# New durations for three kinds of operation in the planner that orders a fused attention and feed-forward kernel, and new due times

## The chip, the cores and the metric

The kernel runs on one core of one Trainium2 chip. The metric is device time in microseconds (us) of one execution. A core has five engines with a queue each: TensorE (PE, with its weight loads listed apart as PEld), VectorE (DVE), ScalarE (ACT), GpSimd (POOL) and SyncE (SP, which here only issues DMAs). An engine works its own queue in order; engines meet through semaphores. The kernel before takes 650.52 us, the median of three runs from 650.5 to 650.76 us.

## The reference

Three stages, all in fp32, on 2 x 768 tokens:

```
scores = (q @ k.T) / 8 + bias(distance) ; keep local window of 96 and 8 global columns
a      = softmax(scores)                ; x = a @ v              8 heads of 64
x      = (x @ w_a) * (x @ w_b) @ w_out                           512 -> 1536 -> 512
h      = x @ w_in ; g = h if h >= 1, 0 if h <= -1, else (h + 1)^2 / 4
out    = g @ w_out2                                              512 -> 2048 -> 512
```

The feed-forward weights are float64 arrays. The kernel makes two fp32r tiles of each, a high and a low part, and does every product of these stages as three matmuls (high by high, high by low, low by high).

## The kernel before, in words

**Work.** The 1536 tokens are three tiles of 512. Attention is cut into 24 *units*, eight to a tile: one pair of heads and 256 queries. Here they are numbered 0 to 23 in the order in which they run. A unit has four PE steps: *scores* (L730), a *turn* for each of its two heads (transposes of the softmax rows, L801) and *values* (L818). Between them lie, per unit, four reductions on DVE that read the scores from PSUM (L754), four exponentials on ACT (L766), one addition of four numbers on ACT (L774), a reciprocal on DVE (L777), four *norms* (softmax rows times the reciprocal: L97 on ACT, L99 on DVE or POOL), two copies of the turned rows out of PSUM (L432 on ACT, L434 on DVE), and a split of the values' result into the high and low part of x (a cast, then L693). The q of each unit is scaled first (L97 or L99 too).

**Weights.** Each of 68 weight tiles arrives raw by DMA and goes through seven operations: Abs on ACT (L421), four bit operations on DVE (L422 to L425; the first may go to POOL), a cast to the high part (L432 or L434) and a subtraction for the low part (L427, DVE or POOL).

**Products.** The feed-forward stages are 2460 matmuls of 128 x 128 weights by 512 columns: `early` (L641) does the first 48, for tile 0, interleaved by column block of x, and `run` does the others (L489 and L518).

**What sets the order.** Nothing is scheduled on the chip. While the program is built, `Clock` replays the kernel with a table of durations and writes each queue in the order that this replay reaches. `on` enters an operation with a due time (now plus a slack by kind, `SLACK`) and a duration for each engine that may do it; `one` gives it to the engine that would end first, with a surcharge for DVE (`BIAS`). `write` and `product` advance PE's clock by the modelled length of a step. The loop at L1043 to L1069 chooses between the next product and the next attention step, by how far attention is behind its share (`behind`, `AHEAD`, `LATE`, `RUN`, `OVER`) and in the order of steps in `ORDER`. Before the first product PE gets filler matmuls (L1066) wherever the replay has nothing for it. On the chip the durations are what they are: a duration in the table that is wrong puts an operation at a wrong place or on a wrong engine, and the queues wait for each other there.

**Tables that matter below.** `NORM` and `NORM1` (L63, L64): the norm of 256 and of 128 columns and the scaling of q, 270 and 165 ns on ACT. The duration of Abs (L421): 520 ns. `TURNED` and the length of a turn (L60, L808). `FIRST` (L44): the loads issued before the replay begins. `UNITS` (L704): how many units may be between scores and values, which is also the depth of the row pools.

Of the kernel before, what the change touches and what calls it, by code (L numbers as in the profile page):

```python
# [15 lines left out]
AF = mybir.ActivationFunctionType  # L16
# [4 lines left out]
P = 128  # L21
# [19 lines left out]

NQ = 2

FIRST = ((0, 0), (0, 1), (2, 0), (0, 2), (1, 0), (2, 1), (0, 3), (1, 1), (2, 2), (1, 2), (2, 3))  # L44

AHEAD_QK, AHEAD_V = 4, 3

# [9 lines left out]
MM = 227  # L57


ENTER, TURNED, LEAVE = 95, 174, 107  # L60
COPY = dict(scalar=520, vector=335)
COPY_PS = dict(scalar=478, vector=602)
NORM = dict(scalar=270, vector=262)  # L63
NORM1 = dict(scalar=165, vector=198)  # L64
SUB = dict(vector=602, gpsimd=1225)
CLAMP = dict(vector=335, gpsimd=1883)

BIAS = dict(any=150, weights=400, norm=150, q=150)

HOP = dict(tensor=200, scalar=160, vector=170, gpsimd=120)  # L70
DMA = dict(issue=580, begin=1600, rate=260, end=900)
# [1 line left out]
BEFORE = 5450  # L73

SLACK = dict(
    qk=0, reduce=-1500, exp=1500, share=-3000, norm=-1000, turn=-3000, x=-1000, evac=0, mid=0, y=2000, weights=4500, soon=1900,
)


GAP = dict(first=0, att=3000, later=3966, soon=26)  # L80

AHEAD = 40


RUN, LATE, OVER = 3, 12, 8

ORDER = "stv"


def as_f32(ap):  # L90
    return ap.bitcast(F32)
# [38 lines left out]
class Clock:  # L130
# [7 lines left out]
    def __init__(self, nc):  # L138
        self.nc = nc
        self.now, self.seq, self.events = 0, 0, []  # L140
        self.busy = dict.fromkeys(self.ENGINES, 0)
        self.port = 0
        self.line = []
        self.dma_issue = self.dma_busy = -1 << 20
        self.poll = lambda: None

        self.att = None
# [5 lines left out]
    def on(self, slack, emit, then=None, need=None, port=True, bias="any", **costs):  # L153


        self.seq += 1
        bisect.insort(self.line, (self.now + slack, self.seq, costs, port, BIAS[bias], emit, then, need))

# [35 lines left out]
                gate = at + ns  # L194
        return False

    def dma(self, n, then):
        issued = max(self.dma_issue, self.now)
        self.dma_issue = issued + DMA["issue"]
        self.dma_busy = max(self.dma_busy, issued + DMA["begin"]) + n / DMA["rate"]  # L200
        self.after(self.dma_busy + DMA["end"] - self.now, then)

    def product(self, ns):

        ns += LEAVE if self.att else 0
        self.att = None
        return ns

# [20 lines left out]
class Loads:  # L229
# [34 lines left out]
    def more_raw(self, u, clock):  # L264

        first = max(n for what, n in FIRST if what == 2)
        for n in range(u + NRAW if u else first + 1, u + NRAW + 1):
# [40 lines left out]
    def dma(self, clock, dst, src, then=lambda: None):  # L308
        n = 4
        for k in dst.shape:  # L310
            n *= k
        self.nc.sync.dma_start(dst, src)
        if clock:
            clock.dma(n, then)
        else:
            self.first.append((n, then))

    def begin(self):
        first = {0: self.load, 1: self.load_v, 2: self.load_raw}
        for what, n in FIRST:  # L320
            first[what](n)

    def follow(self, clock):

        clock.now = -BEFORE
        for n, then in self.first:
            clock.dma(n, then)
        clock.now = 0


class Ffn:
# [3 lines left out]
    def __init__(self, ctx, tc, clock, loads, out, half):  # L335
# [27 lines left out]
        self.early_ps, self.begun = [], False  # L363
        self.gap = GAP["first"]
        self.room = dict(ab=2, acc=2, s1=2, s2=2)
# [28 lines left out]
    def prep(self, urgent):  # L394
        clock = self.clock
        u = self.n_prep
        self.n_prep += 1
        r = self.loads.raw(u)
        low, high = r[:, :, 0], r[:, :, 1]
        b = self.p_bits.tile([P, T], U32, tag="bits", name=f"bits{u}")  # L400
        wh, wl = self.slots.pop(0)
        self.used.append(u)
        self.in_flight += 1
        slack = SLACK["soon" if urgent else "weights"]

        def chain(*steps):
            (emit, costs), rest = steps[0], steps[1:]

            def then():
                if rest:  # L410
                    chain(*rest)
                else:
                    self.loads.more_raw(u, clock)
                    self.w[u] = wh, wl
                    self.in_flight -= 1

            clock.on(slack, emit, then, bias="weights", **costs)

        shl, shr, both, or_ = ALU.logical_shift_left, ALU.logical_shift_right, ALU.bitwise_and, ALU.bitwise_or
        chain(  # L420
            (lambda e: e.activation(as_f32(b), as_f32(high), AF.Abs), dict(scalar=520)),  # L421
            (lambda e: e.tensor_scalar(as_f32(b), as_f32(b), HUGE, TINY, ALU.min, ALU.max), CLAMP),  # L422
            (lambda e: e.tensor_scalar(b, b, 3, 0x3FFFFFF8, shl, both), dict(vector=335)),
            (lambda e: e.scalar_tensor_tensor(b, low, 29, b, shr, or_), dict(vector=602)),  # L424
            (lambda e: e.scalar_tensor_tensor(b, high, 0xC0000000, b, both, or_), dict(vector=602)),  # L425
            (lambda e: self.copy(e, wh, as_f32(b)), COPY),
            (lambda e: e.tensor_tensor(wl, as_f32(b), as_f32(wh), ALU.subtract), SUB),  # L427
        )
# [181 lines left out]
    def prepare(self):  # L610

        if self.can_prep() and self.n_prep in self.loads.have:
            urgent = self.first_use[self.n_prep] - self.now < GAP["soon"]
            if urgent or self.clock.now - self.prep_at >= self.gap:
# [42 lines left out]
class Attention:  # L657
# [15 lines left out]
    def write(self, ns, then, turn=False):  # L673

        if not turn:
            ns += {None: ENTER, "turn": TURNED, "other": 0}[self.clock.att]
        self.clock.att = "turn" if turn else "other"
        self.clock.after(ns + HOP["tensor"], then)
        self.clock.advance(ns)
# [18 lines left out]
class Window(Attention):  # L698
# [2 lines left out]

    UNITS = 3  # L704

    def __init__(self, ctx, early, tc, clock, ffn, loads, ident, masks, scales):
        super().__init__(ctx, tc, clock, ffn, ident)
# [36 lines left out]
    def reduce(self, st, j, r, ps):  # L744
# [34 lines left out]
        def norms():  # L779
            for jj in range(2):  # L780
                for rr in range(NQ):
                    clock.on(SLACK["norm"], *self.norm(st, jj, rr), bias="norm", gpsimd=457, **(NORM if self.places(st)[rr][1] > P else NORM1))

# [11 lines left out]
    def turn(self, st, j):  # L795

        clock, pt = self.clock, st["p", j]
        n = sum(w for _, w in self.places(st))
        ps = self.take()
        for c in range(0, n, P):  # L800
            self.nc.tensor.transpose(ps[:, c : c + P], pt[:, c : c + P], self.ident)  # L801

        def out():
            self.give(ps)
            st["turned", j] = True

        copy = lambda e: self.ffn.copy(e, pt[:, :n], ps[:, :n])
        self.write(146 + 52 * n // P, lambda: clock.on(SLACK["turn"], copy, out, None, False, scalar=20 + n * 9 // 10, vector=n * 7 // 6), True)  # L808

    def values(self, st):  # L810

# [18 lines left out]
    def steps(self):  # L830
# [6 lines left out]
        def score(n):  # L837
            self.scores(units[n])
            if n + 1 < len(units):
                nxt = units[n + 1]  # L840
                here = lambda: nxt.update(qs=True)
                scale = lambda e: loads.scale(e, n + 1, self.scales)
                self.clock.on(SLACK["qk"], scale, here, lambda: "here" in nxt, bias="q", gpsimd=453, **NORM)

# [127 lines left out]
def tile_kernel(ctx: ExitStack, tc: tile.TileContext, nn, qz, k2, qd, kd, vd, wu, out):  # L972
# [54 lines left out]
    with tc.If(near != 0, preferred_fallthrough_block=True) as cmp:  # L1027
        with ExitStack() as arm:
# [14 lines left out]
            while holds:  # L1043
# [4 lines left out]
                if step and (  # L1048
# [4 lines left out]
                    if done == per_tile:  # L1053
                        ffn.gap = GAP["att"]
                    if not any(steps.values()):
# [134 lines left out]
```

## Time and profile before

| | |
|---|---|
| time, median of 3 runs | 650.52 us |
| the profiled execution | 650.85 us |
| its span, first to last instruction | 648.9 us |
| around the span | 1.95 us |
| PE busy | 637.9 us (98%) |
| DVE busy | 444.3 us (68%) |
| ACT busy | 262.1 us (40%) |
| POOL busy | 62.9 us (10%) |

The shares are means over stretches with different limits: attention is in the first 130 us, and from there on the products have PE to themselves. PE's busy time counts filler matmuls and overlapped ends as well. A row of a timeline gives the start, the duration, the engine, the line, the operation and its tiles; where instructions of one engine overlap at their ends, the time that one costs the engine is the distance from its start to the next one's start.

### The profile page before, as it was taken

How to read it: one execution, taken by the hardware profiler on the slowest of the kernel's cores; microseconds unless marked ns; L12 is line 12 of the kernel's file. 1: busy time of each engine (PE TensorE's matmuls, PEld its weight loads, DVE VectorE, ACT ScalarE, POOL GpSimd, SP SyncE). 2: the span in 40 equal slices, each digit the busy share in tenths (PEclk: the TensorE clock that was granted, in tenths of full speed). 3: DMA queues.
4: the chain of work that ended last, by engine and by line, in shares of the span. 5: the costliest groups of instructions: out<-in, count | busy, mean ns of one | idle time of the engine just before them, and what ended most of it. 6: DMA issues, size and time to landing. Idle time of an engine off the chain costs nothing.

```text
span 648.9 us, 8928 instructions
## 1 busy us (share of the span) xinstructions
PE 637.9 (98%) x3211; PEld 516.0 (80%) x3211; DVE 444.3 (68%) x970; ACT 262.1 (40%) x611; POOL 62.9 (10%) x82
## 2 busy tenths in 40 slices
PE   8899999999999999999999999999999999999997
PEld 4567777888888888888888888888888888888886
DVE  7999976364943838943949978685879587744442
ACT  6999989723421213301313435452434133211110
POOL 1112211000000000000000011000010211022220
PEclk9999999999999999999999999999999999999999
DMA  7776652022320303410302411230213120000112
GB/s 241 224 227 197 203 150 87 17 66 66 106 89 0 130 0 98 130 32 1 129 2 88 130 43 66 66 97 33 65 66 96 35 66 0 1 0 17 48 51 86
DMA packets 23765, 52.70 MB, mean 81 GB/s; under 512 B 3104, under 2 KB 11552, under 8 KB 23712
## 3 DMA queue, kind: packets, MB, share of 16 engines
q1 hardware_dynamic: 23568, 52.05, 26.0%
q8 instruction: 27, 0.44, 0.3%
q14 instruction: 26, 0.21, 0.1%
q10 hardware_dynamic: 144, 0.00, 0.0%
HBM read 48.89 MB, written 3.15 MB: 80 GB/s over the span
## 4 chain that ended last, share of the span: by engine, by line
PE 88%; ACT 2%; issue 0%; DVE 0%; ACTq 0%
PE ps L489 48%; PE o L518 20%; PE y L518 15%; PE at L801 2%; PE at L818 2%; PE at L730 1%; ACT p L766 1%; ACT p L432 0%; ACT p L97 0%; PE e L641 0%; ACT bits L421 0%; DVE ab L549 0%; ACT w_hlh L432 0%; ACT a L432 0%; DVE opart L607 0%
## 5 line engine op out<-in xcount | busy, mean ns | idle before, releaser
L566 ACT ACTIVATE c<-c,half 128x512 f32<-128x512 f32 x48 | 34.7, 724 | 139.1 <-DVE c L563 139.0
L489 PE MATMUL ps<-xlx,w_hlh 128*128 128x512 f32 x224 | 87.5, 390 | 0.0
L489 PE MATMUL ps<-xhx,w_hlh 128*128 128x512 f32 x224 | 87.4, 390 | 0.0
L489 PE MATMUL ps<-xhx,w_hll 128*128 128x512 f32 x224 | 87.4, 390 | 0.0
L563 DVE TENSOR_SCALAR c<-ps 128x512 f32<-128x512 f32 x48 | 33.0, 688 | 51.6 <-PE ps L489 51.5
L489 PE MATMUL ps<-xhy,w_hlh 128*128 128x512 f32 x168 | 65.4, 389 | 0.0
L489 PE MATMUL ps<-xly,w_hlh 128*128 128x512 f32 x168 | 65.4, 389 | 0.0
L489 PE MATMUL ps<-xhy,w_hll 128*128 128x512 f32 x168 | 65.4, 389 | 0.0
L549 DVE TENSOR_TENSOR ab<-ps,a 128x512 f32<-128x512 f32 x34 | 23.4, 687 | 56.5 <-PE ps L489 56.3
L432 ACT CAST w_hlh<-bits 128x512 fp32r<-128x512 f32 x50 | 31.0, 622 | 49.4 <-DVE bits L425 44.8
L571 DVE TENSOR_TENSOR g<-ps,c 128x512 f32<-128x512 f32 x48 | 33.0, 688 | 25.1 <-ACT c L566 24.8
L489 PEld LDWEIGHTS ps<-xhx,w_hlh 128*128 128x128 f32 x224 | 42.0, 188 | 9.0 <-issue 0.3
L489 PEld LDWEIGHTS ps<-xhx,w_hll 128*128 128x128 f32 x224 | 42.1, 188 | 8.9 <-issue 0.2
L489 PEld LDWEIGHTS ps<-xlx,w_hlh 128*128 128x128 f32 x224 | 42.1, 188 | 8.7 <-issue 0.2
L421 ACT ACTIVATE bits<-raw 128x512 f32<-128x512 f32 x68 | 43.9, 668 | 8.6 <-DVE w_hll L427 5.3
L425 DVE SCALAR_TENSOR_TENSOR bits<-raw,bits 128x512 uint32<-128x512 uint32 x68 | 46.3, 691 | 0.6
L424 DVE SCALAR_TENSOR_TENSOR bits<-raw,bits 128x512 uint32<-128x512 uint32 x68 | 45.7, 683 | 0.5
L432 ACT COPY a<-ps 128x512 f32<-128x512 f32 x22 | 12.9, 589 | 81.2 <-PE ps L489 81.0
L518 PE MATMUL o<-w_hlh,midl 128*128 128x512 f32 (+1 forms) x101 | 39.1, 387 | 0.0
L518 PE MATMUL o<-w_hll,midh 128*128 128x512 f32 (+1 forms) x101 | 39.1, 387 | 0.0
L518 PE MATMUL o<-w_hlh,midh 128*128 128x512 f32 (+1 forms) x101 | 39.1, 387 | 0.0
L427 POOL TENSOR_TENSOR w_hll<-bits,w_hlh 128x512 fp32r<-128x512 f32 x11 | 14.8, 1350 | 235.4 <-ACT w_hlh L432 212.1
(316 smaller groups left out, 1392.6 us busy)
## 6 DMA issues: line engine op xcount, KB each, us to landing
raw<-in_wu SPq DMA_DIRECT2D x68, 512.0 KB, 3.6
v<-in_vd SPq DMA_DIRECT2D x16, 256.0 KB, 3.0
k<-in_k SPq DMA_DIRECT2D x16, 200.0 KB, 2.9
q<-in_qd SPq DMA_DIRECT2D x48, 64.0 KB, 3.6
out<-opart SPq DMA_DIRECT2D x11, 256.0 KB, 2.0
k<-in_k SPq DMA_DIRECT2D x8, 128.0 KB, 3.6
v<-in_vd SPq DMA_DIRECT2D x8, 128.0 KB, 3.7
v<-in_vd SPq DMA_DIRECT2D x8, 64.0 KB, 2.7
```

What stands on the lines that cost most here:

```text
L421: (lambda e: e.activation(as_f32(b), as_f32(high), AF.Abs), dict(scalar=520)),
L424: (lambda e: e.scalar_tensor_tensor(b, low, 29, b, shr, or_), dict(vector=602)),
L425: (lambda e: e.scalar_tensor_tensor(b, high, 0xC0000000, b, both, or_), dict(vector=602)),
L427: (lambda e: e.tensor_tensor(wl, as_f32(b), as_f32(wh), ALU.subtract), SUB),
L432: e.copy(dst, src)
L489: nc.tensor.matmul(ps, l, r, start=c == 0 and m == 0, stop=last)
L518: nc.tensor.matmul(ps[:, cols], l, r[:, cols], start=f == lo and m == 0, stop=last)
L549: e.tensor_tensor(ab[0], ps, self.a.pop((t, f)), ALU.mult)
L563: e.tensor_scalar(c[0], ps, -1.0, 1.0, ALU.max, ALU.min)
L566: e.activation(c[0], c[0], AF.Square, bias=self.half, scale=0.5)
L571: e.tensor_tensor(g[0], ps, c[0], ALU.max)
L801: self.nc.tensor.transpose(ps[:, c : c + P], pt[:, c : c + P], self.ident)
```

## The change

Line numbers of the changed kernel are 2 to 5 higher. It does five things: it sets the durations of ACT's scaled copy and of Abs higher and models the turns differently, it sets the due times and some limits anew, it issues one raw weight tile less before the replay (`FIRST`), it lets four units be under way (`UNITS`), and it brings in a second DMA queue that stays unused (`ALONG = 0`, so `queue` is always that of SP).

```diff
-FIRST = ((0, 0), (0, 1), (2, 0), (0, 2), (1, 0), (2, 1), (0, 3), (1, 1), (2, 2), (1, 2), (2, 3))
+FIRST = ((0, 0), (0, 1), (2, 0), (0, 2), (1, 0), (2, 1), (0, 3), (1, 1), (1, 2), (2, 2))
+ALONG = 0
-ENTER, TURNED, LEAVE = 95, 174, 107
+ENTER, LEAVE, TURNED = 95, 107, 25
-NORM = dict(scalar=270, vector=262)
-NORM1 = dict(scalar=165, vector=198)
+NORM = dict(scalar=400, vector=262)
+NORM1 = dict(scalar=292, vector=198)
-BIAS = dict(any=150, weights=400, norm=150, q=150)
+BIAS = dict(any=150, weights=150, norm=400, q=150)
...
-    qk=0, reduce=-1500, exp=1500, share=-3000, norm=-1000, turn=-3000, x=-1000, evac=0, mid=0, y=2000, weights=4500, soon=1900,
+    qk=400, reduce=0, exp=1500, share=-3000, norm=0, turn=-3000, x=1000, evac=1000, mid=2000, y=2000, weights=1500, soon=1900,
...
-AHEAD = 40
-RUN, LATE, OVER = 3, 12, 8
-ORDER = "stv"
+AHEAD = 16
+RUN, LATE, OVER = 1, 24, 8
+ORDER = "tsv"
...
-        ns += LEAVE if self.att else 0
+        ns += {None: 0, "turn": TURNED, "other": LEAVE}[self.att]
...
+            queue = sum(q for _, _, q in self.first) < ALONG and len(self.first) % 2
+            (self.nc.scalar if queue else self.nc.sync).dma_start(dst, src)
...
-            (lambda e: e.activation(as_f32(b), as_f32(high), AF.Abs), dict(scalar=520)),
+            (lambda e: e.activation(as_f32(b), as_f32(high), AF.Abs), dict(scalar=560)),
...
-            ns += {None: ENTER, "turn": TURNED, "other": 0}[self.clock.att]
+            ns += 0 if self.clock.att == "other" else ENTER
...
-    UNITS = 3
+    UNITS = 4
...
-        self.write(146 + 52 * n // P, lambda: clock.on(SLACK["turn"], copy, out, None, False, scalar=20 + n * 9 // 10, vector=n * 7 // 6), True)
+        self.write(109 * n // P, lambda: clock.on(SLACK["turn"], copy, out, None, False, scalar=20 + n * 9 // 10, vector=n * 7 // 6), True)
```

**Where instructions go.** In all, 24 fewer operations of the window path stand in ACT's queue, 14 fewer in DVE's, and 38 more in POOL's. Three places show how.

ACT's queue from unit 1's addition (`st_2_0`) on, before. `p_2_0` and `p_0_1` are the softmax rows of units 1 and 2 (the last number is the head), `q_71` the q of unit 3, `bits` a weight tile in preparation, `at` a PSUM bank of attention:

```order
L774 ACTIVATE st_2_0__296<-st_2_0__296 128x4
L766 ACTIVATE p_0_1_0_331,st_0_1__330<-p_0_1_0_331,st_0_1__330 128x256
L97 ACTIVATE q_71<-q_71,scales 128x256
L97 ACTIVATE p_2_0_0_297<-p_2_0_0_297,st_2_0__296 128x256
L97 ACTIVATE p_2_0_1_298<-p_2_0_1_298,st_2_0__296 128x256
L421 ACTIVATE bits_362<-raw_62 128x512
L766 ACTIVATE p_0_1_1_332,st_0_1__330<-p_0_1_1_332,st_0_1__330 128x128
L766 ACTIVATE p_0_1_1_332,st_0_1__330<-p_0_1_1_332,st_0_1__330 128x256
L432 COPY p_2_0_0_297<-at_264 128x512
L774 ACTIVATE st_0_1__330<-st_0_1__330 128x4
```

The same place in the changed kernel:

```order
L779 ACTIVATE st_2_0__296<-st_2_0__296 128x4
L771 ACTIVATE p_0_1_0_330,st_0_1__329<-p_0_1_0_330,st_0_1__329 128x256
L771 ACTIVATE p_0_1_1_331,st_0_1__329<-p_0_1_1_331,st_0_1__329 128x128
L771 ACTIVATE p_0_1_1_331,st_0_1__329<-p_0_1_1_331,st_0_1__329 128x256
L426 ACTIVATE bits_361<-raw_62 128x512
L779 ACTIVATE st_0_1__329<-st_0_1__329 128x4
L99 ACTIVATE p_2_0_1_298<-p_2_0_1_298,st_2_0__296 128x256
L437 COPY p_2_0_0_297<-at_265 128x512
L99 ACTIVATE p_0_1_0_330<-p_0_1_0_330,st_0_1__329 128x128
L99 ACTIVATE p_0_1_0_330<-p_0_1_0_330,st_0_1__329 128x256
L99 ACTIVATE p_0_1_1_331<-p_0_1_1_331,st_0_1__329 128x256
```

The scaling of q and one of unit 1's norms have left the queue, and unit 2's exponentials stand ahead of the norm that remains; unit 2's norms follow close by.

POOL's queue from its first operation inside the window path, before:

```order
L99 TENSOR_SCALAR p_2_0_0_297<-p_2_0_0_297,st_2_0__296 128x256
L422 TENSOR_SCALAR bits_362<-bits_362 128x512
L99 TENSOR_SCALAR p_0_1_0_331<-p_0_1_0_331,st_0_1__330 128x256
L99 TENSOR_SCALAR p_2_1_0_394<-p_2_1_0_394,st_2_1__393 128x256
L99 TENSOR_SCALAR p_2_1_1_395<-p_2_1_1_395,st_2_1__393 128x256
L99 TENSOR_SCALAR p_0_2_0_479<-p_0_2_0_479,st_0_2__478 128x256
L99 TENSOR_SCALAR q_71<-q_71,scales 128x256
L427 TENSOR_TENSOR w_hll_212<-bits_492,w_hlh_211 128x512
```

The same place in the changed kernel:

```order
L101 TENSOR_SCALAR q_70<-q_70,scales 128x256
L101 TENSOR_SCALAR p_0_0_0_277<-p_0_0_0_277,st_0_0__276 128x256
L101 TENSOR_SCALAR p_2_0_0_297<-p_2_0_0_297,st_2_0__296 128x256 x2
L101 TENSOR_SCALAR p_2_0_1_298<-p_2_0_1_298,st_2_0__296 128x256
L432 TENSOR_TENSOR w_hll_205<-bits_309,w_hlh_204 128x512
L101 TENSOR_SCALAR p_0_1_1_331<-p_0_1_1_331,st_0_1__329 128x128
L101 TENSOR_SCALAR q_69<-q_69,scales 128x256
L101 TENSOR_SCALAR p_2_1_0_387<-p_2_1_0_387,st_2_1__386 128x256
L101 TENSOR_SCALAR p_2_1_1_388<-p_2_1_1_388,st_2_1__386 128x256
```

The norms of unit 0 to 3 that left ACT and DVE, and more of the q scalings, are on POOL now, two or three in a row, and so is the subtraction of the first weight tile (`w_hll`).

PE's queue from the last scores ahead of unit 6's turns to its first values (`p_0_3`), before. The `e` tiles are the PSUM banks of the first 48 products, `xhx` and `xlx` the two parts of x:

```order
L730 MATMUL at_264<-k_75,q_68 128x256
L801 MATMUL at_263<-ident,p_0_3_0_554 128x128 x3
L641 MATMUL e_273<-xhx_1_366,w_hlh_205 128x512
L641 MATMUL e_273<-xlx_1_367,w_hlh_205 128x512
L641 MATMUL e_273<-xhx_1_366,w_hll_206 128x512
L801 MATMUL at_265<-ident,p_0_3_1_555 128x128 x3
L641 MATMUL e_274<-xhx_1_366,w_hlh_207 128x512
L641 MATMUL e_274<-xlx_1_367,w_hlh_207 128x512
L641 MATMUL e_274<-xhx_1_366,w_hll_208 128x512
L818 MATMUL at_263<-p_0_3_0_554,v_82 64x128
```

The same place in the changed kernel, from the first of these turns on:

```order
L806 MATMUL at_262<-ident,p_0_3_0_530 128x128 x3
L646 MATMUL e_274<-xhx_0_364,w_hlh_208 128x512
L806 MATMUL at_265<-ident,p_0_3_1_531 128x128 x3
L646 MATMUL e_274<-xlx_0_365,w_hlh_208 128x512
L735 MATMUL at_263<-k_76,q_69 128x128
L735 MATMUL at_262<-k_76,q_69 128x128
L735 MATMUL at_263<-k_76,q_69 128x256
L735 MATMUL at_262<-k_76,q_69 128x256
L823 MATMUL at_265<-p_0_3_0_530,v_82 64x128
```

Six products stood between and behind the two turns, and two stand there now; a unit's scores have moved in behind the turns. Up to unit 6's first values PE has had 18 products before and has had 8 now.

## Rows read from the trace of the kernel before

**Rows 1.** Windows: busy us (and instructions) of each engine, clock, DMA

```profile
6.00:22.00 16.00, 13.67 (x114) 9.35 (x113) 13.84 (x55) 14.94 (x54) 1.58 (x3) 1.00 0.84 263
22.00:30.00 8.00, 7.42 (x58) 4.92 (x58) 7.91 (x35) 7.95 (x28) 1.86 (x4) 1.00 0.86 277
30.00:100.00 70.00, 67.97 (x515) 50.14 (x516) 62.69 (x209) 66.87 (x217) 13.65 (x17) 1.00 0.65 188
130.00:640.00 510.00, 510.00 (x2252) 422.25 (x2251) 339.90 (x590) 145.44 (x236) 41.44 (x32) 1.00 0.19 59
```

**Rows 2.** Groups by line: filler matmuls, count, busy us, mean ns

```profile
L1066 PE MATMUL e<-ident 128*128 128x256 bf16 x21 | 3.3, 274 | 0.0
```

**Rows 3.** Waits of PE, 6 to 130 us: total us, times, longest

```profile
PE at L730 <- ACT q L97: 1.6, 2, 1.0
PE at L801 <- ACT p L97: 1.5, 3, 0.6
PE at L818 <- ACT p L432: 1.1, 3, 0.5
PE at L801 <- DVE xlx L693: 0.5, 1, 0.5
```

**Rows 4.** Timeline of ACT: operations that start one behind another

```profile
14.26 0.50 ACT L97 ACTIVATE q<-q,scales 128x256 f32<-128x256 f32 x1
14.66 0.90 ACT L97 ACTIVATE p<-p,st__296 128x256 f32<-128x256 f32 x2
...
18.48 1.10 ACT L97 ACTIVATE p<-p,st__330 128x128 f32<-128x128 f32 x3
19.47 0.50 ACT L766 ACTIVATE p<-p,st__393 128x256 f32<-128x256 f32 x1
...
19.96 0.36 ACT L432 CAST xhx<-at 128x256 fp32r<-128x256 f32 x1
20.21 0.48 ACT L432 COPY p<-at 128x384 f32<-128x384 f32 x1
```

**Rows 5.** Timeline: additions of units 0 and 15 on ACT

```profile
9.70 0.19 ACT L774 ACTIVATE st__277<-st__277 128x4 f32<-128x4 f32 x1
...
77.40 0.24 ACT L774 ACTIVATE st__1104<-st__1104 128x4 f32<-128x4 f32 x1
```

**Rows 6.** Timeline of PE: first scores, then values of units 6 and 15

```profile
5.74 1.34 PE L730 MATMUL at<-k,q 64*128 64x128 f32 x8
...
40.90 1.01 PE L818 MATMUL at<-p,v 128*64 128x128 f32 x12
...
82.37 0.88 PE L818 MATMUL at<-p,v 128*64 128x128 f32 x12
```

**Rows 7.** Timeline of PE: a turn, values, scores, each with what follows

```profile
42.70 0.66 PE L801 MATMUL at<-ident,p 128*128 128x128 f32 x4
...
43.11 0.48 PE L641 MATMUL e<-xhx,w_hlh 128*128 128x512 f32 x1
...
46.34 1.09 PE L818 MATMUL at<-p,v 128*64 128x128 f32 x16
...
47.36 1.13 PE L730 MATMUL at<-k,q 64*128 64x256 f32 x8
...
48.42 1.09 PE L818 MATMUL at<-p,v 128*64 128x128 f32 x16
```

**Rows 8.** Chain that ended last: start, us, twelve products in a row

```profile
181.53 2.72 PE y L518 x12
```

**Rows 9.** Line 99, norms on POOL and DVE: ns min/median/max, starts

```profile
L99 DVE TENSOR_SCALAR p<-p,st__277 x2: 287/318/348, 10.2 to 10.4; 128x128 f32<-128x128 f32 x1, 128x256 f32<-128x256 f32 x1
...
L99 POOL TENSOR_SCALAR p<-p,st__393 x2: 482/482/482, 23.3 to 23.8; 128x256 f32<-128x256 f32 x2
```

**Rows 10.** Timeline of POOL and DVE: a subtraction and a norm

```profile
78.23 1.43 POOL L427 TENSOR_TENSOR w_hll<-bits,w_hlh 128x512 fp32r<-128x512 f32 x1 [4.79 <-ACT w_hlh L432]
...
78.43 1.31 DVE L99 TENSOR_SCALAR p<-p,st__1104 128x128 f32<-128x128 f32 x1
```

More of the change, by code (lines that the diff above doesn't have):

```diff
@@ L75 @@
 SLACK = dict(
-    qk=0, reduce=-1500, exp=1500, share=-3000, norm=-1000, turn=-3000, x=-1000, evac=0, mid=0, y=2000, weights=4500, soon=1900,
+    qk=400, reduce=0, exp=1500, share=-3000, norm=0, turn=-3000, x=1000, evac=1000, mid=2000, y=2000, weights=1500, soon=1900,
 )
-GAP = dict(first=0, att=3000, later=3966, soon=26)
-AHEAD = 40
-RUN, LATE, OVER = 3, 12, 8
-ORDER = "stv"
+GAP = dict(first=0, att=1610, later=3966, soon=40)
+AHEAD = 16
+RUN, LATE, OVER = 1, 24, 8
+ORDER = "tsv"
 def as_f32(ap):
@@ L143, in __init__ @@
         self.line = []
-        self.dma_issue = self.dma_busy = -1 << 20
+        self.dma_issue, self.dma_busy = [-1 << 20] * 2, -1 << 20
         self.poll = lambda: None
@@ L195, in one, with dma @@
         return False
-    def dma(self, n, then):
-        issued = max(self.dma_issue, self.now)
-        self.dma_issue = issued + DMA["issue"]
+    def dma(self, n, then, queue=0):
+        issued = max(self.dma_issue[queue], self.now)
+        self.dma_issue[queue] = issued + DMA["issue"]
         self.dma_busy = max(self.dma_busy, issued + DMA["begin"]) + n / DMA["rate"]
@@ L311, in dma @@
             n *= k
-        self.nc.sync.dma_start(dst, src)
         if clock:
+            self.nc.sync.dma_start(dst, src)
             clock.dma(n, then)
         else:
-            self.first.append((n, then))
+            queue = sum(q for _, _, q in self.first) < ALONG and len(self.first) % 2
+            (self.nc.scalar if queue else self.nc.sync).dma_start(dst, src)
+            self.first.append((n, then, queue))
     def begin(self):
@@ L325, in follow @@
         clock.now = -BEFORE
-        for n, then in self.first:
-            clock.dma(n, then)
+        clock.dma_issue[1] = clock.now + DMA["issue"]
+        for n, then, queue in self.first:
+            clock.dma(n, then, queue)
         clock.now = 0
```

## The prediction, as it went on record before the changed kernel ran

> **What bounds the kernel now.** I read the windows first, then the waits of PE, then the timelines of ACT and PE. From 130 to 640 us PE is busy 510.00 of 510 us at the full clock [rows 1], and twelve products take 2.72 us, 0.227 us each [rows 8]. There is nothing to win there. What can be won lies before 130 us: PE idles 2.33 us from 6 to 22, 0.58 to 30 and 2.03 to 100 us [rows 1], and it spends 21 filler matmuls on top [rows 2]. Its longest recorded waits name ACT: for a scaled q 1.6 us, for norms 1.5, for copies 1.1; DVE has one of 0.5 [rows 3].
>
> ACT is full there: 14.94 of 16 us, then 7.95 of 8 [rows 1]. To see how full, I add up ACT's queue in order, each operation by the distance from its start to the next one's: a q or a norm of 256 columns 0.40 us (14.26 to 14.66), two norms of 128 and one of 256 together 0.99 (18.48 to 19.47), so 0.29 for 128, an exponential of 256 with its sum 0.49 (19.47 to 19.96), a cast of half an x tile 0.25 (19.96 to 20.21) [rows 4]. By that count unit 0's addition ends after 3.15 us of work and unit 15's after 70.0. The trace has the ends at 9.80 and 77.50 (start plus 0.10) [rows 5]. The difference goes from 6.65 to 7.5, so between these two points ACT stood still for 0.9 us in 68. ACT's own work sets the pace of attention up to about 80 us.
>
> The same count for PE: 1.06 us for a unit's scores (47.36 to 48.42), 1.02 for values (46.34 to 47.36), 0.41 for a turn of four blocks (42.70 to 43.11) [rows 7], 0.227 for a product, and 0.1 to 0.2 for each change from products into a step. PE's first step starts at 5.74, unit 6's values at 40.90, unit 15's at 82.37 [rows 6]. Its own work up to these is 25.1 and 64.3 us, so it had lost 40.90 - 5.74 - 25.1 = 10.1 us by the one and 82.37 - 5.74 - 64.3 = 12.3 us by the other. ACT's work up to the addition of the same unit leads PE's work up to its values by 28.6 - 25.1 = 3.5 us at unit 6 and 70.0 - 64.3 = 5.7 us at unit 15, the highest of the 24. The loss grows by 2.2 us between the two, and so does the lead: PE loses what ACT's lead demands.
>
> **The change part by part.**
>
> *Norms, q and Abs in the planner.* The replay took 0.27 us for a norm or q of 256 columns on ACT and 0.165 for one of 128, where the trace has 0.40 and 0.29 [rows 4], so it gave ACT too much and placed PE's steps too early. With the right numbers the order takes work off ACT. Up to the addition of unit 6: two norms of 256 (0.80), two of 128 (0.58), four q (1.60) and three casts (0.75) fewer, 3.7 us of 28.6, which leaves 24.9. PE's work up to unit 6's values falls as well, since ten products (2.27) move behind them and one unit's scores (1.06) come ahead, with fewer entries into steps: 25.1 becomes 23.5. The lead falls from 3.5 to 1.4 us. Up to unit 15: ACT 62.9 instead of 70.0 (six norms of each width, four q, six casts fewer, the rest within 0.4), while PE has 94 products behind it instead of 77 and 69.7 us of work: the lead is -6.8. The highest lead of the new order is the 1.4 at unit 6. As long as ACT is the releaser, the loss at unit 6 is 10.1 - 2.1 = 8.0 us, and it does not grow behind it. Against 12.3 that is **-4.3 us**.
>
> *What comes late next.* ACT's waits go; behind them stand the chain of a unit (addition, reciprocal, norms, turn, copies) and the other engines. Norms move to POOL, where one takes 0.48 us [rows 9] against 0.40 on ACT, two or three in a row, and a turn waits for the last. I give back the two longest kinds of wait that the new order can bring under another name, 0.6 for a norm and 0.5 for a split [rows 3], in sum **+1.1 us**, an estimate between 0 and the whole 4.3.
>
> *PE's own work.* The same scores, turns, values and products are issued. Fillers fall from 21 to 18, but they fill time that is lost anyway. PE changes from products into attention 22 times instead of 23, and further on a unit's scores follow a turn directly instead of the reverse; by the distances above that is **-0.3 us**, between -0.6 and 0.
>
> *Turn length, ENTER, LEAVE, TURNED, AHEAD, ORDER, RUN, LATE, OVER.* They act only through PE's order, which is counted above. Attention of the second tile now ends at product 94 of the 96 before its first use instead of 77. What is late next is the split of unit 15: its last column block is read by the eleventh product behind its values, 2.5 us later, and a cast and a subtraction (0.25 and about 0.35 us) with their hops go in between. The third tile's attention ends at product 216, 24 before its use. Cost nothing; without that cover 1 us each.
>
> *UNITS, FIRST, ALONG.* Four units under way give more softmax rows room and no work. One raw tile less is loaded ahead; its Abs stands at 21.3 us of ACT work, near 28 us, and its DMA is queued on SP behind unit 7's k. If it came late, ACT would wait behind it; I count nothing, up to +1 us. The second queue is not used. From 130 us on each weight tile's last bit operations stand as far ahead of their product as before; the tail is the same row by row.
>
> *Sum.* -4.3 + 1.1 - 0.3 = -3.5 us against the profiled execution's 650.85 (span 648.9 plus 1.95): 647.35. Its median runs were 0.33 lower, so **647.0 us**. With the bounds: nothing given back and -0.6 on PE make 645.6; all given back makes 650.2.
>
> **The port that POOL and DVE share.** A DVE norm of 128 columns takes 0.29 us, but 1.31 beside a POOL subtraction of 1.43, and ends close behind it [rows 9, 10]. The Trainium skill (SBUF — State Buffer, "Who interferes with whom") says that VectorE and GpSimd share one pair of ports, that whoever starts first holds it for the whole instruction, and that the other blocks. The trace agrees, 1.31 against 0.29. The rule speaks against a change that puts 38 more operations on POOL, and it is the slower rival below.
>
> **The rivals.**
> - *The waits come back.* Attention is ahead of the products in the new order, so early on PE has fewer products to fill a wait with: 8 instead of 18 up to unit 6. If the loss behind unit 6 is again 2.2 us, as it was, only the 2.1 at unit 6 remain: 650.52 - 2.1 - 0.3 = 648.1. For it: before the first product nothing but fillers can cover. Against it: ACT's lead falls everywhere, by 7 us and more from unit 15 on.
> - *DVE takes over.* DVE is nearly as full, 13.84 of 16, 7.91 of 8 and 62.69 of 70 us [rows 1]. Up to the second split of unit 7 its count falls from 37.0 to 33.4 us (norms and subtractions leave, splits and reductions come), and PE's work to these values falls from 29.9 to 26.6: the lead only goes from 7.1 to 6.8. If DVE sets the pace there, -0.3 - 0.3 = -0.6: 649.9, no change. Against it: hardly a wait of PE names DVE, and the products that read this split come much later.
> - *Slower: POOL holds DVE up.* Up to unit 7's norms POOL works about 13.3 us instead of 5.9, by the durations above. If all of the 7.4 us more held DVE, DVE's lead of 6.8 would become 14.2; the 2.3 us that DVE idled up to 30 us [rows 1] pay for part. That is -0.3 + 7.4 - 2.3 = +4.8, with PE's -0.3 a time of 655.0. It decides from 2.6 us of hold-up on. Against it: 26 instead of 40 DVE operations up to there read SBUF alone, and the replay keeps the two apart.
>
> **How the numbers follow.** The forecast, 645.6 to 649, gets 0.60; the returning waits (648.1) 0.18; DVE (649.9) 0.13; POOL's hold-up (650.6 to 655) 0.09. About 0.2%, 1.3 us, is what can be told from no change. Faster by more than that: the first two, 0.78. Within: 0.13. Slower: 0.09. The range is 645.2 to 650.2 us: the full gain with a little more, to DVE's case and the end at which all is given back.
>
> **What would show it.** In the changed profile ACT's busy time in 30 to 100 us should fall below 64 us and POOL's rise by some 7; PE's waits for q and norms on ACT should go from 3.1 us to under 1.5; unit 6's values should start near 37 to 38 us (5.74 + 23.5 + 8) with 8 products done, and PE should be full behind it. The forecast is wrong if unit 6's values start later than 39.5, if PE's waits name DVE or POOL for over 3 us, or if PE idles at all behind 130 us.

## The result and the profile after

The changed kernel takes 645.31 us, the median of four runs from 644.88 to 645.42; the kernel before took 650.64 us beside it. The ratio is 0.9915, with a 95% interval from 0.9898 to 0.9932: 5.3 us faster. That is the direction forecast, but 1.7 us below the forecast of 647.0. As a time, 645.31 is 0.1 us above the low end of the range, 645.2; as a ratio, 0.9915 lies just under that end, which is 645.2 / 650.52 = 0.9918. The profiled execution took 644.88 us, its span is 643.1. Of two kernels below, *ACT early* and *old BIAS*, half of the runs had a granted TensorE clock of 0.995 to 0.997 over the whole run and were some 1.4 us longer than their other runs at 0.998 to 1.000, whose medians are 646.98 and 650.15 us.

The windows of the changed kernel, in the stretches of [rows 1] (busy us and instructions of PE, PEld, DVE, ACT, POOL, then clock, DMA share, GB/s):

```profile
6.00:22.00 16.00, 14.35 (x123) 9.26 (x125) 14.11 (x63) 15.10 (x54) 5.31 (x9) 1.00 0.84 252
22.00:30.00 8.00, 7.37 (x60) 4.80 (x57) 7.39 (x33) 8.00 (x31) 6.49 (x12) 1.00 0.96 291
30.00:100.00 70.00, 69.16 (x549) 54.51 (x549) 63.37 (x215) 66.44 (x214) 21.59 (x37) 1.00 0.68 203
130.00:640.00 510.00, 508.25 (x2265) 420.88 (x2263) 339.38 (x592) 144.16 (x233) 44.00 (x33) 1.00 0.19 60
```

PE gains 0.68 us of busy time from 6 to 22 us and 1.19 from 30 to 100, nothing from 22 to 30. Behind 130 us it is as full as before: the 1.75 us that the last row lacks lie behind the last product, which starts at 637.97 us. ACT is as full as it was, and POOL works 16 us more up to 100 us. The fillers [rows 2] are 18 instead of 21:

```profile
L1071 PE MATMUL e<-ident 128*128 128x256 bf16 x18 | 3.0, 274 | 0.0
```

PE's waits from 6 to 130 us, all that are listed, against [rows 3]:

```profile
PE at L735 <- DVE q L101: 0.9, 2, 0.5
PE at L735 <- POOL q L101: 0.7, 1, 0.7
PE at L806 <- DVE p L439: 0.5, 1, 0.5
PE at L735 <- DVE st__728 L759: 0.3, 1, 0.3
PE at L806 <- ACT p L99: 0.2, 1, 0.2
PE at L806 <- POOL q L101: 0.2, 1, 0.2
```

Before, ACT was named for 4.2 us; now for 0.2, and DVE and POOL for 2.6. PE's timeline shows where these stand (first scores, the values of unit 6, and the one step that waits long behind 36 us):

```profile
5.76 1.00 PE L735 MATMUL at<-k,q 64*128 64x128 f32 x8
...
36.15 0.88 PE L823 MATMUL at<-p,v 128*64 128x128 f32 x12
...
41.13 0.48 PE L735 MATMUL at<-k,q 64*128 64x128 f32 x2 [0.52 <-DVE q L101]
41.88 0.92 PE L735 MATMUL at<-k,q 64*128 64x128 f32 x6 [0.26 <-DVE st__728 L759]
```

**What PE loses, counted one way for all kernels.** From the first scores to the start of the last product I take the filler stretches, and for each pair of neighbouring matmuls what goes beyond the usual distance of such a pair (the lower quartile over the traces). Before: 621.3 us of its own work, 5.5 of filler stretches, 11.3 of waits. After: 620.5, 3.5 and 8.3. Of the 5.9 us, 2.0 are fillers, 3.0 waits and the rest, some 0.9, PE's own work. Below, "loss" is fillers and waits together, by 44 us, by 100 us and at the end:

| | by 44 | by 100 | end |
|---|---|---|---|
| before | 10.7 | 14.6 | 16.7 |
| after | 9.0 | 9.9 | 11.7 |

Three of the 5.0 us of loss that went lie between 44 and 100 us, where the changed kernel loses 0.9 us and the old one 3.9.

### The profile page after: what moved, and what is told of

It reads as the page before. It is cut to its first block, busy times and chain, and to the rows that moved or that the text cites. A ratio compares the mean times of both kernels' runs of the same rounds, so it can differ in the third digit from the quotient of the medians.

```text
span 643.1 us, 8972 instructions
## 1 busy us (share of the span) xinstructions
PE 633.8 (99%) x3208; PEld 515.6 (80%) x3208; DVE 437.8 (68%) x956; ACT 254.8 (40%) x587; POOL 84.0 (13%) x120
## 4 chain that ended last, share of the span: by engine, by line
PE 95%; ACT 2%; DMA 1%; DVE 0%; issue 0%; POOL 0%; ACTq 0%; POOLq 0%; DVEq 0%
PE ps L494 49%; PE o L523 20%; PE y L523 15%; PE at L735 3%; PE at L823 3%; PE at L806 3%; PE e L646 1%; ACT p L771 1%; PE warm_ps L993 1%; DMA v<-in_vd 1%; ACT p L437 0%; ACT p L99 0%; DVE p L759 0%; ACT bits L426 0%; POOL q L101 0%
## 5 line engine op out<-in xcount | busy, mean ns | idle before, releaser
L432 POOL TENSOR_TENSOR w_hll<-bits,w_hlh 128x512 fp32r<-128x512 f32 x13 | 17.9, 1374 | 247.1 <-DVE w_hlh L439 147.7
L437 ACT COPY a<-ps 128x512 f32<-128x512 f32 x27 | 15.8, 585 | 85.7 <-PE ps L494 85.6
L437 ACT CAST w_hlh<-bits 128x512 fp32r<-128x512 f32 x43 | 26.7, 621 | 48.0 <-DVE bits L430 48.0
L759 DVE CUSTOM_DVE_ANT_0 p<-at,masks 128x256 f32<-128x256 f32 (+1 forms) x96 | 32.9, 394 | 11.9 <-PE at L735 10.8
```

Of the source, the lines that this page charges most:

```text
L437: e.copy(dst, src)
L759: e.tensor_tensor_reduce(pt, ps[:, at : at + w], self.masks.m[:, m0 : m0 + w], scale=-(0.5 ** (2 * st["p"] + j + 1)), scalar=3e38, op0=ALU ...
```

## The experiments

Theory A is the prediction's: ACT's highest lead over PE's own work (ACT's work up to a unit's addition, less PE's up to its values) sets what PE loses, one us for one. Its rivals stand with each group. Loss is given as above (by 44 / by 100 / end).

**One half of the change, and ACT's load in an order that stays.** Theory B: the order of PE's steps, the turn lengths and the fourth unit make the gain, whatever ACT's lead.

Kernel before, with the three durations alone:

```diff
-NORM = dict(scalar=270, vector=262)
-NORM1 = dict(scalar=165, vector=198)
+NORM = dict(scalar=400, vector=262)
+NORM1 = dict(scalar=292, vector=198)
-            (lambda e: e.activation(as_f32(b), as_f32(high), AF.Abs), dict(scalar=520)),
+            (lambda e: e.activation(as_f32(b), as_f32(high), AF.Abs), dict(scalar=560)),
```

> The kernel before with only the planner's durations of ACT's norm, q and Abs set to those of the change. Theory A (ACT's lead sets PE's loss): the time PE loses before its products run alone is about 7.1 us plus the highest lead of ACT's work over PE's own, as in both kernels (12.9 us lost at a lead of 5.7, 8.4 at 1.4). By its order the highest lead here is 3.6 and PE's own work 0.4 more than in the changed kernel: 645.3 + 2.2 + 0.4 = 647.9 us. Theory B (the gain comes from the order of PE's steps, the turn's length and the fourth unit, which are all undone here): no gain, 650 us or more.

651.12 us, ratio 1.0006 (0.9997 to 1.0016): nothing gained, and A's number missed by 3 us. Loss 9.8 / 12.7 / 16.3. The first 44 us did improve; 2.0 us went between 60 and 70 us, where PE waits for DVE, and 1.9 at 142 us. There the new order put the last unit's turn and values next to each other, with nothing between (PE's timeline):

```profile
141.66 1.03 PE L801 MATMUL at<-ident,p 128*128 128x128 f32 x8
142.99 1.57 PE L818 MATMUL at<-p,v 128*64 128x128 f32 x16 [0.29 <-ACT p L432]
145.02 0.50 PE L489 MATMUL ps<-xhx,w_hlh 128*128 128x512 f32 x1 [0.46 <-ACT xhx L432]
145.48 0.50 PE L489 MATMUL ps<-xlx,w_hlh 128*128 128x512 f32 x1
```

The values wait for the copy of the turn, the next product for the split of the values. In the changed kernel nine products stand between this turn and its values.

The changed kernel with the old durations (the same diff, reversed):

> The changed kernel with only the planner's durations of ACT's norm, q and Abs set back. By its order ACT's highest lead is 6.7 us (unit 8), PE's own work 0.5 less. Theory A: 645.3 + 5.3 - 0.5 = 650.1 us. Theory B: the steps keep their order, so 645.3 to 646.5 us.

653.16 us, 1.0034 (1.0022 to 1.0047): all of the gain gone, and 2.2 us more than the kernel before that ran beside it (650.93). B falls; A has the direction, and is 3 us short. Loss 11.2 / 17.1 / 19.1.

The order of before with ACT's 16 scalings of q issued on POOL, and the changed order with POOL's q issued on ACT:

```diff
-                scale = lambda e: loads.scale(e, n + 1, self.scales)
+                scale = lambda e: loads.scale(self.nc.gpsimd if e is self.nc.scalar else e, n + 1, self.scales)
```

> The kernel before, its order unchanged in every queue's rest, but the 16 scalings of q that stand on ACT are issued on POOL in their place. ACT's highest lead falls from 5.7 to 3.0 us (unit 4) and PE's own work stays. Theory A: the loss falls by 2.7 us, 647.9 us, and PE's waits for q are no longer for ACT. Theory B: no gain, 650 to 651 us.

> The changed kernel, its order unchanged in every queue's rest, but the scalings of q that stand on POOL are issued on ACT in their place. ACT's highest lead rises from 1.4 to 3.9 us (unit 14). Theory A: the loss grows by 2.5 us, 647.8 us. Theory B: 645.3 to 645.8 us, since PE's order is the same.

649.01 us, 0.9970 (0.9958 to 0.9983), and 647.23 us, 0.9945 (0.9929 to 0.9962). With the order held, ACT's load moves the time both ways, by 1.9 us each, where A had 2.7 and 2.5. The q itself comes at another time too in these two; the next group leaves that out.

**A known amount of work, in the changed order.** Theory C: the first 40 us belong to DVE and POOL, or to transfers. Eight operations that nobody reads, behind the exponentials or the minima of two units, written to a tile of their own. The edit of *ACT early*, in the main; *ACT late* names units 15 and 16, and *DVE early* has a scaled copy behind the minima of units 4 and 5:

```diff
             e.activation(pt, pt, AF.Exp, bias=most, scale=-1.0, accum_out=total)
+            if st["n"] in (4, 5):
+                e.activation(self.extra, self.ident, AF.Copy, scale=0.5)
```

> The changed kernel, in its order unaltered, with 8 extra copies of 128x128 on ACT that nobody reads, four behind the exponentials of unit 4 and four behind those of unit 5 (about 24 us). At 0.29 us each they are 2.3 us of ACT's work. Theory A (until about 42 us ACT is never idle, and its lead over PE's own work sets what PE loses): the lead at unit 6 goes from 1.4 to 3.7 us and all of the 2.3 us reaches the end, 647.2 to 647.7 us. Theory C (the first 40 us are set by DVE and POOL, or by the transfers, and ACT is busy only because it is fed evenly): under 0.8 us, below 646.1.

> The changed kernel with the same 8 extra copies on ACT, now behind the exponentials of units 15 and 16 (about 75 us), where ACT's lead over PE's own work is -6.8 us. Theory A: they are hidden whole, 645.0 to 645.7 us. Theory C makes no difference between early and late: as much as the early ones cost, to within 0.5 us.

> The changed kernel with 8 extra scaled copies of 128x128 on DVE that nobody reads, behind the four masked minima of units 4 and 5. At 0.20 us each they are 1.6 us of DVE's work. Theory A: DVE has 1.9 us of idle time between 6 and 22 us and is not the limit, so under half of it reaches the end, 645.3 to 646.1 us. Theory C: DVE is the limit, and 1.2 to 1.6 us reach the end, 646.5 to 646.9.

One of them costs ACT less than I had said, 0.20 us from its start to the next (ACT's timeline, the first of the eight):

```profile
23.30 0.30 ACT L774 ACTIVATE extra<-ident 128x128 f32<-128x128 f32 x1
23.50 0.51 ACT L772 ACTIVATE p<-p,st__464 128x256 f32<-128x256 f32 x1
```

So ACT got 1.6 us more each time. On DVE six of the eight cost 0.13 to 0.14 us each and the two beside longer work on POOL 0.34 and 0.87, 2.0 us in all (DVE's timeline, the longest):

```profile
24.14 0.95 DVE L765 TENSOR_SCALAR extra<-ident 128x128 f32<-128x128 f32 x1
25.01 0.41 DVE L760 CUSTOM_DVE_ANT_0 p<-at,masks 128x256 f32<-128x256 f32 x1
```

ACT early: 647.70 us (646.88 to 648.36), 0.9956 (0.9939 to 0.9973), 2.4 us above the changed kernel by the medians and 2.0 by the profiled runs; the loss at the end grows by 1.6, the whole dose, and nearly all of it by 36 us. ACT late: 646.13 us, 0.9927 (0.9910 to 0.9943), 0.8 more; in the trace 0.75 us appear between 70 and 80 us, so where the lead is -6.8 us half of the dose still reached PE. Each unit's extra operations stand ahead of its own norms, for which its turn waits; that this is the reason was not tried. Another 0.4 us lie ahead of the first of them: by so much two traces differ in any case. DVE early: 646.52 us, 0.9936 (0.9920 to 0.9953), 1.2 more, of which A had allowed 0.8 and which C had. In the first 36 us both queues pass their work on to PE. A single engine's lead is not enough of a theory.

**One set of numbers put back at a time.** Theory S (with B2 for the first): only the durations with AHEAD and LATE matter.

```diff
-AHEAD = 16
+AHEAD = 40
-RUN, LATE, OVER = 1, 24, 8
+RUN, LATE, OVER = 3, 12, 8
-ORDER = "tsv"
+ORDER = "stv"
```

> The changed kernel with four of its numbers put back (AHEAD 40, RUN 3, LATE 12, ORDER stv): which step of PE comes first. All the rest, the three durations among it, is new. ACT's highest lead here is 2.2 us (unit 6 and on), PE's own work to product 300 is 0.45 us less than in the changed kernel. Theory A: 645.7 us, between 645 and 646.8, so these four numbers are not what the change gains by. Theory B2 (the order of PE's own steps is what keeps the later losses away, those behind 44 us of the two experiments with only half of the change): 647.5 to 649.

647.53 us, 0.9950 (0.9934 to 0.9967), loss 10.0 / 11.7 / 14.4. A missed by 1.8 us; B2 had 647.5 to 649. 1.0 us of it lies between 125 and 150 us: there the turns and the values of the last two units stand next to each other.

```diff
-ENTER, LEAVE, TURNED = 95, 107, 25
+ENTER, TURNED, LEAVE = 95, 174, 107
...
-        self.write(109 * n // P, lambda: clock.on(SLACK["turn"], copy, out, None, False, scalar=20 + n * 9 // 10, vector=n * 7 // 6), True)
+        self.write(146 + 52 * n // P, lambda: clock.on(SLACK["turn"], copy, out, None, False, scalar=20 + n * 9 // 10, vector=n * 7 // 6), True)
```

> The changed kernel with the old lengths of a turn and of the changes between products and attention steps in the planner's model. ACT's highest lead over PE's own work is 3.3 us instead of 1.4, PE's own work 0.3 us more. Theory A (the highest lead of ACT sets what PE loses, about one us for one): 647.3 to 647.9 us. Theory S (the gain is made by the durations together with AHEAD and LATE; the other sets are worth nothing on their own): as the changed kernel, 645 to 646.3.

646.17 us, 0.9928 (0.9911 to 0.9945), loss 8.3 / 9.8 / 11.7: the loss is that of the changed kernel, with ACT's lead at 3.3 us. What it has more is PE's own work, 1.2 us. A missed.

```diff
-    UNITS = 4
+    UNITS = 3
```

> The changed kernel with three units under way instead of four. ACT's highest lead is 3.3 us, PE's own work 0.65 us more. Theory A: 647.4 to 648.2 us. Theory S: 645 to 646.3. A third reading (the fourth unit is what lets PE go on while one unit waits, so that the late waits of 44 to 100 us come back): 648.5 and more, with the loss between 44 and 100 us over 2 us where the changed kernel has 0.8.

648.84 us, 0.9972 (0.9962 to 0.9982), loss 10.1 / 12.4 / 14.3: 2.3 us between 44 and 100 us, as the third reading had it.

```diff
-    qk=400, reduce=0, exp=1500, share=-3000, norm=0, turn=-3000, x=1000, evac=1000, mid=2000, y=2000, weights=1500, soon=1900,
+    qk=0, reduce=-1500, exp=1500, share=-3000, norm=-1000, turn=-3000, x=-1000, evac=0, mid=0, y=2000, weights=4500, soon=1900,
-GAP = dict(first=0, att=1610, later=3966, soon=40)
+GAP = dict(first=0, att=3000, later=3966, soon=26)
```

> The changed kernel with the old due times (SLACK and GAP). ACT's highest lead is 4.5 us instead of 1.4. Theory A: 648.0 to 648.8 us, the most of these four. Theory S: 645 to 646.3.

648.42 us, 0.9961 (0.9947 to 0.9976), as A had it. The old `FIRST`:

```diff
-FIRST = ((0, 0), (0, 1), (2, 0), (0, 2), (1, 0), (2, 1), (0, 3), (1, 1), (1, 2), (2, 2))
+FIRST = ((0, 0), (0, 1), (2, 0), (0, 2), (1, 0), (2, 1), (0, 3), (1, 1), (2, 2), (1, 2), (2, 3))
```

> The changed kernel with the old list of first loads: one raw tile more ahead, and one pair swapped. ACT's highest lead is 2.1 us instead of 1.4. Theory A: 645.8 to 646.3 us. Theory S: 645 to 646.3 as well. If a load that comes a place earlier or later on the queue moves the wait for a scaled q at 41 us, the loss of that stretch (36 to 44 us, 1.5 us in the changed kernel) goes up or down by over 0.5 us, and the time with it.

646.23 us, 0.9928 (0.9911 to 0.9944). The stretch from 36 to 44 us loses 0.7 instead of 1.5, the one up to 22 us 0.9 more. S falls with units and due times; each of these five sets is worth 0.9 to 3.5 us alone.

**The planner's replay.** Theory R: once its durations are the traced ones, the replay's own end tells what an order is worth.

```diff
-BIAS = dict(any=150, weights=150, norm=400, q=150)
+BIAS = dict(any=150, weights=400, norm=150, q=150)
```

> The changed kernel with the old BIAS (what DVE is held to cost more for weight pieces and norms). Theory R (the planner's replay is right once its durations are the traced ones, so a change of its numbers costs what the replay's own end says: 633.49 us in the changed kernel, 636.78 here): +3.3, 648.1 to 649.3 us. Theory A (ACT's highest lead over PE's own work, 2.9 us here instead of 1.4, sets the loss): 646.5 to 647.3.

651.02 us, 1.0003 (0.9993 to 1.0013). A missed by 4 us (3 by 650.15); R has the direction, and is 2 us short (1 by 650.15). This comes nearest to the prediction's rival "DVE takes over", in a kernel that keeps the old surcharges; PE's waits name DVE for 1.8 us, ACT for 1.2 and POOL for 1.0. The window of 30 to 100 us has DVE at 68.83 of 70 (63.37 in the changed kernel) and POOL at 14.33:

```profile
30.00:100.00 70.00, 67.96 (x532) 52.67 (x531) 68.83 (x226) 62.35 (x198) 14.33 (x20) 1.00 0.65 197
```

The changed kernel with the old duration of Abs, and with those of the scaled copy:

```diff
-            (lambda e: e.activation(as_f32(b), as_f32(high), AF.Abs), dict(scalar=560)),
+            (lambda e: e.activation(as_f32(b), as_f32(high), AF.Abs), dict(scalar=520)),
```

> The changed kernel with the old duration of Abs alone (0.52 instead of 0.56 us). Theory R: the replay ends at 634.73, +1.2, and is nearly right (0.04 us for each Abs): 646.0 to 647.0 us. Theory A: highest lead 2.6 us, +1.2: the same. If Abs' duration didn't matter: 645.0 to 645.7.

```diff
-NORM = dict(scalar=400, vector=262)
-NORM1 = dict(scalar=292, vector=198)
+NORM = dict(scalar=270, vector=262)
+NORM1 = dict(scalar=165, vector=198)
```

> The changed kernel with the old durations of the scaled copy alone (0.27 and 0.165 us instead of 0.40 and 0.29). Theory R: the replay ends at 634.19, but is short by 0.13 us for each norm and q that it gives ACT (some 20 of them in the first 40 us, 2.6 us, of which two thirds reach PE): 647.0 to 648.5 us. Theory A: highest lead 3.8 us, +2.4: 647.2 to 648.2. If the scaled copy's duration is not what matters: under 646.

646.20 us, 0.9929 (0.9913 to 0.9946), and 648.71 us, 0.9964 (0.9952 to 0.9977). Both theories had the first; the second is 0.2 us over R's range and 0.5 over A's. Of the two the scaled copy counts more: 3.4 us, against 0.9 for Abs. Both put back together cost 7.9 us above, more than the sum. Nor do the eight sets of this and the last group add up to the gain of 5.3 us: they come to some 20. Each says what a set is worth beside all the others as they are now, and not its share of the gain. PE's waits with the old norms name ACT's q again, as [rows 3] did:

```profile
PE at L735 <- ACT q L99: 2.1, 2, 1.5
PE at L823 <- ACT p L437: 0.9, 2, 0.5
```

Two sets found by letting the replay run on many, the first with `BIAS` any 500, weights 0, norm 150, q 50, the second 550, 150, 350, 150; `SLACK` and `GAP` differ as well, and of the rest:

```diff
-AHEAD = 16
-RUN, LATE, OVER = 1, 24, 8
-ORDER = "tsv"
+AHEAD = 20
+RUN, LATE, OVER = 3, 8, 12
+ORDER = "svt"
...
-RUN, LATE, OVER = 1, 24, 8
-ORDER = "tsv"
+RUN, LATE, OVER = 2, 28, 6
+ORDER = "stv"
```

> The changed kernel's durations with numbers found by letting the replay run on many sets of BIAS, SLACK, GAP, AHEAD, RUN, LATE, OVER and ORDER and taking the earliest end, 632.73 instead of 633.49 us. Theory R: -0.8, 644.5 us, between 643.8 and 645.6 (replay and measured time have differed by up to 1 us so far); what is left to win by the order is small. Theory A: the highest lead is the same 1.4 us and PE's own work 0.66 less, 644.7; the two theories agree here, and a time over 646.5 speaks against both.

> A second set of numbers from the same search as e14: the replay ends at 632.84 us instead of the changed kernel's 633.49. If the replay's end is good to about 1 us, as the runs so far say (with traced durations the measured last product lies 4.2 to 6.6 us behind it), this is 645 to 647 us, as e14; under 644.9 it is a better order than the changed kernel's.

646.24 us, 0.9930 (0.9913 to 0.9946), and 645.53 us, 0.9917 (0.9900 to 0.9933): no better than the changed kernel, although the replay put them 0.7 us ahead of it; the first is 0.6 us over R's range. The start of the last product minus the replay's end, over all kernels whose order a replay set:

| durations in the replay | kernels | measured minus replay, us |
|---|---|---|
| traced norms and Abs | after 4.5, steps 4.7, turns 4.8, units 6.4, due times 5.3, first 4.2, BIAS 6.2, searched 6.6 and 6.1, durations alone 6.7 | 4.2 to 6.7 |
| old Abs alone | 4.4 | 4.4 |
| old norms | before 10.7, both old 9.6, old norms alone 8.0 | 8.0 to 10.7 |

The replay ended at 633.12 us for the old order and at 633.49 for the new one. It did not find a better plan; its plan became true.

**The wait at 41 us.** DVE and POOL of the changed kernel there (timelines):

```profile
39.42 1.39 DVE L428 TENSOR_SCALAR bits<-bits 128x512 uint32<-128x512 uint32 x1
40.73 0.34 DVE L101 TENSOR_SCALAR q<-q,scales 128x256 f32<-128x256 f32 x1
...
39.25 1.27 POOL L432 TENSOR_TENSOR w_hll<-bits,w_hlh 128x512 fp32r<-128x512 f32 x1 [1.85 <-DVE w_hlh L439]
```

The chain of waits puts this q down to a transfer instead:

```profile
37.40 3.35 DMA v<-in_vd
40.75 0.32 DVE q L101
```

```diff
-            (lambda e: e.tensor_tensor(wl, as_f32(b), as_f32(wh), ALU.subtract), SUB),
+            (lambda e: (self.nc.vector if u == 3 else e).tensor_tensor(wl, as_f32(b), as_f32(wh), ALU.subtract), SUB),
```

> The changed kernel with one instruction moved: POOL's subtraction of the fourth weight tile (39.25 us, 1.27 us long) is issued on DVE, where it stands behind the scaled q and a reciprocal. In the changed kernel DVE's bit operation beside it took 1.39 us instead of 0.42, and the q behind it, for which PE waits at 41 us, started at 40.73. Theory P (POOL's subtraction held DVE up): the bit operation takes 0.42 us again, q starts near 39.8, PE's loss between 36 and 44 us falls from 1.5 to 0.5 to 1.0, and the time is 0.4 to 0.9 us shorter than the changed kernel's, 644.4 to 645.0 us, if nothing else is late. Theory D (that q waits for its load, which the chain of waits puts at 40.75 us): q starts at 40.7 as before and nothing is won, 645.2 to 646.0.

DVE's timeline with that subtraction moved:

```profile
39.57 0.42 DVE L428 TENSOR_SCALAR bits<-bits 128x512 uint32<-128x512 uint32 x1
39.90 0.35 DVE L101 TENSOR_SCALAR q<-q,scales 128x256 f32<-128x256 f32 x1
40.16 0.17 DVE L782 RECIPROCAL st__629<-st__629 128x4 f32<-128x4 f32 x1
40.25 0.66 DVE L432 TENSOR_TENSOR w_hll<-bits,w_hlh 128x512 fp32r<-128x512 f32 x1
```

The bit operation takes 0.42 us, the q starts 0.83 us earlier, and PE's wait for it is gone; 0.47 us for the minimum behind it remain. P holds, and the chain's DMA was not the cause. Loss from 36 to 44 us: 1.1 instead of 1.5, a little over P's 0.5 to 1.0. 644.75 us, 0.9906 (0.9889 to 0.9922): the fastest kernel here, but the intervals of the two overlap almost whole, so the 0.6 us are shown by the trace in part and by the times not at all.

## Why the prediction was right or wrong

**ACT's lead, -4.3 us: the number came, in part by luck.** Unit 15's values start at 83.46 us: 83.46 - 5.76 - 69.7 is a loss of 8.0 us, the figure forecast, against 12.3. The way there was another one. At unit 6 the loss was 36.15 - 5.76 - 23.5 = 6.9 us, 1.1 less than forecast, so the values came earlier than the 37 to 38 us named; from there to unit 15 it grew by 1.1, where the lead had nothing, and the wait at 41 us is most of that. Two errors of 1.1 us cancel in the 8.0. That ACT has no time to spare held: it idled 0.2 us between 9 and 42 us.

**The loss, -4.3 + 1.1 = -3.2 us: the step that failed.** It went wrong in two places. The loss at unit 6 was sized by ACT's work up to the addition alone, as if the way from there to the values stayed as long. The addition did come 4.0 us earlier (3.7 forecast), but the values 4.75. The 0.8 us between the two are the wait of the reciprocal behind the addition (timelines of before and then of after):

```profile
35.48 0.23 ACT L774 ACTIVATE st__553<-st__553 128x4 f32<-128x4 f32 x1
...
36.71 0.17 DVE L777 RECIPROCAL st__553<-st__553 128x4 f32<-128x4 f32 x1
```

```profile
31.52 0.21 ACT L779 ACTIVATE st__529<-st__529 128x4 f32<-128x4 f32 x1
...
31.95 0.17 DVE L782 RECIPROCAL st__529<-st__529 128x4 f32<-128x4 f32 x1
```

Before, DVE had a copy and a minimum to end first and began the reciprocal 1.2 us behind the addition's start; now 0.4 us behind it. From the reciprocal to the values both take 4.2 us. This is read from two traces; no run tried it. The other place is the +1.1 us given back: two waits for a norm and a split, put on top of the lead's 8.0 us. A wait of that size did come (the q at 41 us), but inside the 8.0 and not on top of them; by the end nothing was given back. The old kernel also lost 0.5 us more behind unit 15, nearly all of it in a wait for ACT's norm at 83.25 us, which the new one does not. The loss fell by 5.0 us, where the sum had 3.2.

**PE's own work: mis-sized.** -0.9 us instead of -0.3, and outside the bounds of -0.6 and 0. I counted the distances of a few kinds of change; the count over all neighbouring matmuls has them. That the turn lengths act through PE's order alone was right in kind, but they alone change it by 1.2 us (the old turns).

**Together** 1.8 + 0.6 = 2.4 us between the sum's 3.5 and the 5.9 of the traces: the profiled executions are 650.85 and 644.88 us.

**Was the lead the reason?** Only in part. Over the sixteen kernels of this study without added work or the moved subtraction, loss and highest lead correlate at 0.80, with a slope of 1.1 us per us. But single kernels lie 2 us and more off the line: old turns (lead 3.3, loss 11.7) and old BIAS (2.9, 15.8). What the runs support is wider: the replay believed ACT to be faster than it is, so it planned steps of PE for times at which ACT, and behind it DVE and POOL, had not delivered; with the traced norms the plan is 4 to 7 us short instead of 8 to 11. The other numbers had to be set anew to that replay, since the durations alone gain nothing.

**The rivals.** "The waits come back" happened by half: from unit 6 to unit 15 the changed kernel lost 1.1 us and the old one 2.2, but the start had gained more than the rival allowed. "DVE takes over" comes nearest when BIAS stays old; the new one sends norms to POOL. "POOL holds DVE up" is real, and once delays a q for PE, by 0.8 us; but it is no more than before. Between 6 and 100 us four DVE operations beside POOL's work ran 0.15 us or more over the usual duration of their kind, 1.5 us in all; in the kernel before it was three, with 2.1 us. The Trainium skill (SBUF — State Buffer, "Who interferes with whom") has VectorE and GpSimd share ports, with the one that comes second blocked for the other's whole instruction. The trace agrees: 1.39 us beside POOL's subtraction against 0.42 without it.

**The signs named.** POOL's busy time from 30 to 100 us rose by 7.9 (7 forecast): right. PE's waits for q and norms on ACT fell to 0.2 us: right. Those that name DVE or POOL sum to 2.6, under 3. PE does not idle behind 130 us before its last product: right. Unit 6's values come with 8 products done: right. PE was to be full behind them and waited 0.8 us at 41 us: wrong. ACT's busy time in 30 to 100 us was to fall below 64 us and is 66.44: wrong. ACT's whole busy time did fall, from 262.1 to 254.8 us, but more of it is done by 100 us; what falls is the stretch from 100 to 124, from 20.65 to 14.08 us (windows of before and then of after, columns as above):

```profile
100.00:124.00 24.00, 24.00 (x179) 18.84 (x174) 12.60 (x55) 20.65 (x67) 1.89 (x4) 1.00 0.22 68
```

```profile
100.00:124.00 24.00, 24.00 (x171) 19.55 (x171) 7.93 (x29) 14.08 (x40) 3.25 (x7) 1.00 0.08 23
```

**Open:** why with traced durations the measured end still lies 4.2 to 6.7 us behind the replay, and why this differs by 2.5 us from order to order. Whatever makes that difference decides among the best orders, and the replay can't see it. No run here has numbers searched with the old durations, so how near they could come without the new ones is not shown.

## What to carry to other kernels

Where an order is planned, hold the planner's durations against the trace before tuning its weights: one that was 0.13 us short on the fullest engine was worth 3.4 us here beside the other new numbers, and correcting it paid only once the other numbers were tuned to it. The lead of one engine's queue over another's sizes a large gap; below some 2 us the chain of a single unit, the other queues and the last unit of a stage, which has nothing behind it to hide a wait, decide. Count the way behind the fullest engine's last operation in the new order as well, and not that engine's work alone. A wait that you expect to come back may lie inside the loss already counted: don't add it on top.

## What was not expected of the hardware

A scaled copy of 128x128 from one tile to another with a constant scale costs ACT 0.20 us from its start to the next start, where a norm of the same width, in place and with a scale from a tile, costs 0.29 [rows 4]. Its row shows 0.30 us; read by that alone, the eight would be 2.4 us instead of 1.6.
